# A fused attention, channel mixer and expert kernel: where gathers, output copies, transposes and index products stand in the order of work

## The chip, the cores and the metric

The kernel runs on one core of a Trainium2 chip. The metric is the device time of one execution in microseconds (us), from three runs of the same program. A profile of one further execution shows every instruction of the core's engines: PE (matrix products; PEld is its loading of the stationary operand), DVE, ACT and POOL (elementwise work), and the queues SP (plain transfers) and POOL (indirect transfers, those with a list of row numbers).

## The reference

Three stages follow one another on 4 batches of 576 tokens with 512 channels. The first is attention with 8 heads, in which scores further than `tau` below a row's maximum are dropped. The second adds a low-rank mix over tokens and a two-layer channel network:

```python
xt = x.transpose(0, 2, 1)
u = x + (xt @ U @ V).transpose(0, 2, 1)
x = u + np.maximum(u @ w_ch1, 0.0) @ w_ch2
```

The third sends each token to one of 8 experts (512 to 1024 to 512). A gate decides whether a token takes its own best expert or the expert of the token before it, so the choice runs along the tokens:

```python
fresh_e = int(np.argmax(logits[b, s]))
e = fresh_e if s == 0 or local_gate[b, s] < 0.5 else prev_e
out[b, s] = p[e] * (np.maximum(x[b, s] @ w1[e], 0.0) @ w2[e])
```

## The kernel before

**Stages.** Batch 0's attention runs alone. Then attention of batch b is interleaved with the channel network of batch b - 1 (`channel`, lines 633 to 642). At the end `channel(B - 1)`, the channel network of the last batch, runs interleaved with `early_slots` (line 886), which already plans two expert units from the first three batches' tokens. Then come the last batch's logits, the store of its rows to the DRAM buffer `ydram` (`store_rows`), its routing (`route`), the plan of the remaining units (`late_slots`) and the experts (`experts`, line 1127).

**Precision.** Every float32 product is made of three products of split operands: a high part, made by ACT (`h` in the names), and a remainder, made by DVE or POOL (`l`). So each weight chunk of 128x512 needs one ACT copy and one subtraction. For the channel weights (`load_w`, line 583) POOL makes all remainders: `w0l` and `w1l`, for the 16 slices f of the hidden layer. High and remainder parts of the first layer have two rooms (`W0`), those of the second five (`W1`). For the expert weights (`Chunks.split_to`, line 993) POOL makes one chunk's remainder in four (`k % 4 == 1`, line 1002), DVE the others. An expert unit has 16 chunks. Two of them share a raw buffer, which the SP queue refills for the next unit once both are split.

**Units and slots.** A slot is a list of up to 128 tokens of one expert, and a unit is one expert with one to three slots: unit 0 has 3, unit 1 has 2, the units after them 3, 3, 2, 2, 2, 2, 1, 1. `slot_rows` (line 817) makes the lists: for two groups of tokens at a time DVE builds a one-hot row matrix `r1` (96 tokens x 128 rows, line 858) and a narrow matrix `rh` with two columns for each slot (lines 861 to 867: the token number and the gate's probability). PE multiplies them into one PSUM bank, `pi` (line 869), over 18 token groups for units 0 and 1 (names ending in a) and 24 for the rest (ending in b). The narrow matrix is the stationary operand, so the result has a list in each row. It is copied (line 872), transposed by PE (line 874), copied again (line 878) and turned into integers (`idx`).

**A unit's way.** `gather` (line 1019) fetches a slot's rows from `ydram` by an indirect transfer on POOL's queue, into one of the six `wr` buffers, which the channel weights use too. `columns` (line 1037) transposes them on PE (`split_t`, line 1028): four transposes into one PSUM bank, then an ACT copy for the high part and a DVE subtraction for the remainder. Units 0 and 1 use the one bank `tp` of the pool `px`; later units use the two `mm` banks. `layer1` and `layer2` follow. `layer1` writes its sums to two `l1` banks in turn, so its third group has to wait until DVE has made the remainder of the first (`h_0l`, line 1074). `layer2` keeps one `l2` bank for each slot; there are three. Then each slot is scaled by DVE into an output tile `o` of 512 columns (line 1123), which takes one of two `yr` buffers, and written to the output by an indirect transfer on POOL's queue (line 1124). The third slot's `o` needs the buffer of the first, so it waits until that transfer has landed.

**Order.** Each engine takes its instructions strictly in the order in which they were queued. A planner works that order out beforehand from its own estimates of time: it takes the earliest-traced instruction that its clock holds to be ready. In the experts only SP keeps the order of the program. An instruction given to `keep_in_program_order` is queued behind the instruction traced last before it on its engine; this is order in the queue alone, no wait for an end.

The lines that matter for tracing order: all channel weights are traced before `experts`. There `gather(0)` is first, then `columns(0)`, then `gather(1)`, then unit 0's layer 1, in which unit 0's chunks are split. Of a channel slice `w0l` is traced before `w1l`, so the last POOL instruction traced before the gathers is `w1l` of slice 15.

Of the kernel before, what the change touches and what calls it, by code (L numbers as in the profile page):

```python
# [83 lines left out]
def attention_channel_moe(ctx, tc, qk, vv, tau, umat, vrep, wch, wgl, wexp, consts, out):  # L84
# [732 lines left out]
    def slot_rows(nm, nt, s0, s1):  # L817
# [29 lines left out]
            dve.tensor_reduce(out=slot, in_=sb, axis=AX.X, op=ALU.add)  # L847
        dve.tensor_tensor(out=slot, in0=slot, in1=q, op=ALU.add)
        bk = mm_tile if s0 else lambda n: px_tile("l2", n)
        pi = bk(f"pi{nm}")[:2 * n, :128]  # L850
        G = 2
        for j in range(0, nt, G):
            c = slice(j, j + G)
            bc = lambda x: x.unsqueeze(2).to_broadcast([CH, G, n])
            rf = me.tile([CH, G * 2 * NSLOT], F32, tag="rh", name=f"rh{nm}_{j}", bufs=2)
            rh = rf[:, :G * 2 * n].rearrange("p (g t s) -> p g t s", g=G, t=2)
            r1 = me.tile([CH, G, 128], F32, tag="r1", name=f"r1{nm}_{j}", bufs=2)
            dve.tensor_tensor(out=r1, in0=row[:, c].unsqueeze(2).to_broadcast([CH, G, 128]),
                              in1=cst[:CH, C_I128:C_I128 + 128].unsqueeze(1).to_broadcast([CH, G, 128]),
                              op=ALU.is_equal)  # L860
            for a, z, code in ((0, n, s0),) if s0 else ((0, FIRST[0], CODES[0]), (FIRST[0], EARLY, CODES[1])):
                m = z - a
                dve.tensor_tensor(out=rh[:, :, 1, a:z], in0=slot[:, c].unsqueeze(2).to_broadcast([CH, G, m]),
                                  in1=cst[:CH, C_SLOT + code:C_SLOT + code + m].unsqueeze(1).to_broadcast([CH, G, m]),
                                  op=ALU.is_equal)
            dve.tensor_tensor(out=rh[:, :, 0], in0=rh[:, :, 1], in1=bc(cst[:CH, C_TOK + j:C_TOK + j + G]), op=ALU.mult)
            dve.tensor_tensor(out=rh[:, :, 1], in0=rh[:, :, 1], in1=bc(p_all[:, c]), op=ALU.mult)
            for i in range(G):
                pe.matmul(pi, lhsT=rf[:, i * 2 * n:i * 2 * n + 2 * n], rhs=r1[:, i],
                          start=(j + i == 0), stop=(j + i == nt - 1))  # L870
        tr = me.tile([2 * NSLOT, 128], F32, tag="tr", name=f"tr{nm}")[:2 * n]
        dve.tensor_copy(tr, pi)
        pt = bk(f"pt{nm}")[:, :2 * n]
        pe.transpose(pt, tr, ident[:2 * n, :2 * n])
        ti = me.tile([128, 2, NSLOT], F32, tag="ti", name=f"ti{nm}", bufs=2)[:, :, :n]
        ii = me.tile([128, 2, NSLOT], F32, tag="ii", name=f"ii{nm}")[:, :, :n]
        idx = me.tile([128, 2, NSLOT], I32, tag="idx", name=f"idx{nm}", bufs=2)[:, :, :n]
        dve.tensor_copy(ti, pt.rearrange("p (a s) -> p a s", a=2))
        dve.tensor_scalar(out=ii[:, 0], in0=ti[:, 0], scalar1=-1.0, scalar2=0.0, op0=ALU.add, op1=ALU.max)
        dve.tensor_scalar(out=ii[:, 1], in0=ti[:, 0], scalar1=0.0, scalar2=OOB, op0=ALU.is_equal, op1=ALU.mult)  # L880
        dve.tensor_tensor(out=ii[:, 1], in0=ii[:, 0], in1=ii[:, 1], op=ALU.add)
# [87 lines left out]
    class Chunks:  # L969
# [23 lines left out]
        def split_to(self, n):  # L993
            while self.done < min(n, len(self.order)):
                s, k = self.order[self.done]
                hi, lo = self.room(f"{s}_{k}")
                self.done += 1
                i = k // 2
                x = raws[i][:, k % 2 * 512:k % 2 * 512 + 512]
                act.activation(hi, x, AF.Copy)  # L1000
                eng = pool if k % 4 == 1 else dve
                eng.tensor_tensor(out=lo, in0=x, in1=hi.bitcast(F32), op=ALU.subtract)  # L1002
                self.parts[s, k] = (hi, lo)
                if k % 2 and s + 1 < self.u1:
                    load_expert(s + 1, i)
# [13 lines left out]
    def gather(u):  # L1019
        for s in UNITS[u]:  # L1020
            yg = mlp.tile([128, DM], F32, tag="wr", name=f"yg{s}", bufs=WR)
            n = (B - 1) * S if s < EARLY else NTOK
            pool.indirect_dma_start(out=yg, out_offset=None, in_=ydram[:n, :],
                                    in_offset=bass.IndirectOffsetOnAxis(ap=ixs[s][0], axis=0),
                                    bounds_check=n - 1, oob_is_err=False)
            rows[s] = yg

    def split_t(name, src, hi, lo, late):

        tp = mm_tile(f"{name}p") if late else px.tile([128, 512], F32, tag="tp", name=f"{name}p")  # L1030
        for d in range(4):
            pe.transpose(tp[:, d * 128:d * 128 + 128], src[:, d * 128:d * 128 + 128], ident)
        t3 = tp.rearrange("p (a b) -> p a b", a=4)
        act.activation(hi, t3, AF.Copy)
        dve.tensor_tensor(out=lo, in0=t3, in1=hi.bitcast(F32), op=ALU.subtract)

    def columns(u):
# [6 lines left out]
        hi, lo = yts[u]  # L1044
        for i, s in enumerate(UNITS[u]):
            c = slice(i * 128, i * 128 + 128)
            split_t(f"y{s}", rows[s], hi[:, :, c], lo[:, :, c], u >= U0)
            yield

    def hidden(u, f):  # L1050
# [53 lines left out]
    def layer2(W, u, hs, nxt):  # L1104
# [14 lines left out]
        for _ in nxt:  # L1119
            pass  # L1120
        for i, s in enumerate(slots):
            o = mlp.tile([128, S], F32, tag="yr", name=f"o{s}", bufs=2)[:, :DM]
            dve.tensor_scalar(out=o, in0=po[i], scalar1=ixs[s][2], scalar2=None, op0=ALU.mult)  # L1123
            pool.indirect_dma_start(out=out, out_offset=bass.IndirectOffsetOnAxis(ap=ixs[s][1], axis=0),  # L1124
                                    in_=o, in_offset=None, bounds_check=NTOK - 1, oob_is_err=False)
# [119 lines left out]
```

## Time and profile before

| | |
|---|---|
| median of 3 runs | 1111.4 us (1111.2 to 1113.02) |
| the profiled execution | 1110.32 us |
| its span, first to last instruction | 1108.5 us |
| mean granted TensorE clock | 0.986 |
| busy share of the span | PE 94%, DVE 62%, ACT 52%, POOL 28% |

The profiled execution is 1.1 us below the median of the runs; 1.8 us of it lie outside the span. [...]

### The profile page before, as it was taken

What the parts mean: (1) busy time and instruction counts of PE and PEld (TensorE: products, weight loads), DVE (VectorE), ACT (ScalarE), POOL (GpSimd) and SP (SyncE); (2) the same over time, 40 slices, a digit from 0 to 9 for tenths busy, and PEclk for the clock granted to TensorE, in tenths of its full rate; (3) what the DMA queues carried; (4) which work ended last, traced back from release to release, by engine and by line L of the source; (5) the groups of instructions that cost most, each with busy time, mean ns of one, the idle gap of its engine ahead of it and who ended that gap; (6) DMA issues with size and microseconds to landing.
All of it is one profiled execution on the core that took longest, in us unless ns stands there. A gap on an engine that the chain in (4) does not pass through costs nothing. (4 is left out here: it accounts for less than half of the span.)

```text
span 1108.5 us, 19450 instructions
## 1 busy us (share of the span) xinstructions
PE 1037.1 (94%) x7170; PEld 910.7 (82%) x7170; DVE 687.5 (62%) x1617; ACT 581.6 (52%) x1220; POOL 313.4 (28%) x246
## 2 busy tenths in 40 slices
PE   6788899999999999999999999999999999999995
PEld 4566788889888889988898998979878788889874
DVE  6898776776465666646656554552458664456573
ACT  5788676674554556546464554332333344445462
POOL 1221123142222314221241222234411433233231
PEclk9899999999999999999999999989999999999998
DMA  6544577762223124132321211352243465456550
GB/s 199 184 152 138 181 247 227 240 214 93 88 92 95 58 78 126 53 99 77 94 70 42 67 49 55 114 213 82 77 138 133 129 222 162 153 175 200 186 170 15
DMA packets 57992, 143.83 MB, mean 130 GB/s; under 512 B 7133, under 2 KB 7901, under 8 KB 57888
## 3 DMA queue, kind: packets, MB, share of 16 engines
q1 hardware_dynamic: 54528, 132.27, 37.4%
q0 software_dynamic: 3360, 10.23, 2.8%
q8 instruction: 58, 0.95, 0.4%
q14 instruction: 46, 0.38, 0.1%
HBM read 124.65 MB, written 18.61 MB: 129 GB/s over the span
## 5 line engine op out<-in xcount | busy, mean ns | idle before, releaser
L610 PE MATMUL l<-uh,w0h 128*128 128x256 f32 (+1 forms) x512 | 157.9, 308 | 4.5 <-DVE hl L614 2.1
L596 POOL TENSOR_TENSOR w1l<-wr,w1h 128x512 fp32r<-128x512 f32 x64 | 81.7, 1299 | 269.7 <-ACT w1h L595 246.2
L627 PE MATMUL l<-hh,w1h 128*128 128x256 f32 (+1 forms) x512 | 157.4, 307 | 0.2 <-DVE yT L630 0.2
L612 PE MATMUL l<-uh,w0l 128*128 128x256 f32 (+1 forms) x512 | 153.7, 300 | 2.8 <-POOL w0l L596 2.8
L596 POOL TENSOR_TENSOR w0l<-wr,w0h 128x512 fp32r<-128x512 f32 x64 | 85.0, 1327 | 243.4 <-ACT w0h L595 233.8
L611 PE MATMUL l<-ul,w0h 128*128 128x256 f32 (+1 forms) x512 | 153.3, 299 | 0.0
L628 PE MATMUL l<-hl,w1h 128*128 128x256 f32 (+1 forms) x512 | 152.8, 298 | 0.0
L629 PE MATMUL l<-hh,w1l 128*128 128x256 f32 (+1 forms) x512 | 152.2, 297 | 0.0
L1000 ACT ACTIVATE eh<-ew 128x512 fp32r<-128x512 f32 x160 | 94.4, 627 | 88.6 <-PE el L1116 46.4
L335 ACT ACTIVATE p<-s,st 128x576 f32<-128x576 f32 x144 | 104.5, 741 | 61.3 <-DVE st L324 61.1
L1002 DVE TENSOR_TENSOR el<-ew,eh 128x512 fp32r<-128x512 f32 x120 | 98.4, 840 | 41.9 <-ACT eh L1000 40.6
L339 DVE SCALAR_TENSOR_TENSOR p<-s,st,p 128x576 f32<-128x576 f32 x144 | 114.6, 815 | 15.2 <-ACT p L335 10.0
L324 DVE TENSOR_REDUCE st<-s 128x1 f32<-128x576 f32 x144 | 105.6, 751 | 28.4 <-PE s L291 26.4
L289 PE MATMUL s<-kh,qs 128*128 128x288 f32 x320 | 99.7, 330 | 17.8 <-DVE p L339 8.4
L388 ACT ACTIVATE ptt<-tp 128x512 f32<-128x512 f32 (+1 forms) x192 | 90.3, 494 | 41.5 <-PE tp L387 41.1
L614 DVE SCALAR_TENSOR_TENSOR hl<-l,hh 128x256 fp32r<-128x256 f32 (+1 forms) x128 | 58.1, 454 | 81.3 <-ACT hh L613 80.6
L630 DVE TENSOR_TENSOR yT<-l,yT 128x256 f32<-128x256 f32 (+1 forms) x128 | 58.2, 455 | 77.9 <-PE l L629 77.4
L610 PEld LDWEIGHTS l<-uh,w0h 128*128 128x128 f32 x512 | 97.4, 190 | 8.3 <-DVE hl L614 3.4
L612 PEld LDWEIGHTS l<-uh,w0l 128*128 128x128 f32 x512 | 97.4, 190 | 4.1 <-POOL w0l L596 3.0
L627 PEld LDWEIGHTS l<-hh,w1h 128*128 128x128 f32 x512 | 97.0, 190 | 3.9 <-issue 2.6
L387 PE MATMUL tp<-cst,p 128*128 128x128 f32 x576 | 94.5, 280 | 5.0 <-ACT ptt L388 4.8
L1002 POOL TENSOR_TENSOR el<-ew,eh 128x512 fp32r<-128x512 f32 x40 | 55.3, 1383 | 153.0 <-ACT eh L1000 133.2
(467 smaller groups left out, 2526.7 us busy)
## 6 DMA issues: line engine op xcount, KB each, us to landing
ew<-in_wexp_dram SPq DMA_DIRECT2D x80, 512.0 KB, 4.3
wr<-wdram SPq DMA_DIRECT2D x128, 256.0 KB, 2.9
cr<-in_wch_dram SPq DMA_DIRECT2D x32, 512.0 KB, 5.0
raw<-in_qk_dram SPq DMA_DIRECT2D x30, 304.0 KB, 3.1
wdram<-w SPq DMA_DIRECT2D x32, 256.0 KB, 2.7
v<-in_vv_dram SPq DMA_DIRECT2D x16, 352.0 KB, 3.1
raw<-in_qk_dram SPq DMA_DIRECT2D x16, 320.0 KB, 3.6
raw<-in_qk_dram SPq DMA_DIRECT2D x17, 288.0 KB, 3.0
```

Source lines behind the costliest of these rows:

```text
L289: pe.matmul(s["t"][:, h, :288], lhsT=qs[:, qc:qc + 128], rhs=kh[:, k0:k0 + 288], start=(j == 0), stop=False)
L324: dve.tensor_reduce(out=self.st[:, 0, h:h + 1], in_=self.t[h], axis=AX.XY, op=ALU.max, negate=True)
L335: act.activation(self.halves(h), self.t[h], AF.Exp, bias=self.st[:, 0, h:h + 1])
L339: dve.scalar_tensor_tensor(out=p, in0=self.t[h], scalar=self.st[:, 1, h:h + 1], in1=p, op0=ALU.is_ge, op1=ALU.mult, accum_out=self.rvs[:, ...
L596: pool.tensor_tensor(out=lo, in0=x, in1=hi.bitcast(F32), op=ALU.subtract)
L610: pe.matmul(pm, lhsT=w1h[:, wk], rhs=uh[:, k, o:o + n], start=(k == 0), stop=False)
L611: pe.matmul(pm, lhsT=w1h[:, wk], rhs=ul[:, k, o:o + n], start=False, stop=False)
L612: pe.matmul(pm, lhsT=w1l[:, wk], rhs=uh[:, k, o:o + n], start=False, stop=(k == 3))
L627: pe.matmul(pm, lhsT=w2h[:, wd], rhs=hh[:, o:o + n], start=(f == f0), stop=False)
L628: pe.matmul(pm, lhsT=w2h[:, wd], rhs=hl[:, o:o + n], start=False, stop=False)
L629: pe.matmul(pm, lhsT=w2l[:, wd], rhs=hh[:, o:o + n], start=False, stop=(f == f0 + 3))
L1002: eng.tensor_tensor(out=lo, in0=x, in1=hi.bitcast(F32), op=ALU.subtract)
```

## The change

It has four parts.

1. In `gather`, unit 0's three gathers are kept in program order on POOL, and so are unit 0's four POOL remainders in `split_to`. The first gather is thereby queued behind `w1l` of slice 15, the first remainder behind the last gather of unit 1, and each of the others behind the one before it.
2. The third slot's output tile gets a buffer of its own in the pool `ma`.
3. The transposes of unit 0 go to the three `l2` banks; unit 1 keeps the bank `tp`, later units the `mm` banks.
4. In `slot_rows` the one-hot rows become the stationary operand and the narrow matrix the moving one. The result has the lists in columns, so the copy of line 872 and the transpose of line 874 with its bank are gone.

```diff
-        pi = bk(f"pi{nm}")[:2 * n, :128]
+        pi = bk(f"pi{nm}")[:, :2 * n]
...
-                pe.matmul(pi, lhsT=rf[:, i * 2 * n:i * 2 * n + 2 * n], rhs=r1[:, i],
+                pe.matmul(pi, lhsT=r1[:, i], rhs=rf[:, i * 2 * n:i * 2 * n + 2 * n],
                           start=(j + i == 0), stop=(j + i == nt - 1))
-        tr = me.tile([2 * NSLOT, 128], F32, tag="tr", name=f"tr{nm}")[:2 * n]
-        dve.tensor_copy(tr, pi)
-        pt = bk(f"pt{nm}")[:, :2 * n]
-        pe.transpose(pt, tr, ident[:2 * n, :2 * n])
...
-        dve.tensor_copy(ti, pt.rearrange("p (a s) -> p a s", a=2))
+        dve.tensor_copy(ti, pi.rearrange("p (a s) -> p a s", a=2))
...
-                eng.tensor_tensor(out=lo, in0=x, in1=hi.bitcast(F32), op=ALU.subtract)
+                x = eng.tensor_tensor(out=lo, in0=x, in1=hi.bitcast(F32), op=ALU.subtract)
+                if s == 0 and eng is pool:
+                    tc.keep_in_program_order(x)
...
-            pool.indirect_dma_start(out=yg, out_offset=None, in_=ydram[:n, :],
+            x = pool.indirect_dma_start(out=yg, out_offset=None, in_=ydram[:n, :],
...
+            if u == 0:
+                tc.keep_in_program_order(x)
...
-        tp = mm_tile(f"{name}p") if late else px.tile([128, 512], F32, tag="tp", name=f"{name}p")
+        tp = {0: lambda n: px_tile("l2", n), 1: lambda n: px.tile([128, 512], F32, tag="tp", name=n)}.get(
+            u, mm_tile)(f"{name}p")
...
-            o = mlp.tile([128, S], F32, tag="yr", name=f"o{s}", bufs=2)[:, :DM]
+            if i < 2:
+                o = mlp.tile([128, S], F32, tag="yr", name=f"o{s}", bufs=2)[:, :DM]
+            else:
+                o = ma.tile([128, DM], F32, tag="o", name=f"o{s}")
```

## Rows read from the trace of the kernel before

**Rows 1.** The page, part 1: busy us, share of the span, instructions.

```profile
PE 1037.1 (94%) x7170; PEld 910.7 (82%) x7170; DVE 687.5 (62%) x1617; ACT 581.6 (52%) x1220; POOL 313.4 (28%) x246
```

**Rows 2.** Timeline, PE, 870 to 980: start, us, engine, instruction [idle before <- releaser].

```profile
877.17 0.38 PE L1069 MATMUL el<-y1h,eh 128*128 128x256 f32 x1 [2.10 <-DVE h_0l L1074]
...
941.86 0.44 PE L1069 MATMUL el<-y3h,eh 128*128 128x384 f32 x1 [1.71 <-DVE h_0l L1074]
...
978.57 0.39 PE L1069 MATMUL el<-y4h,eh 128*128 128x256 f32 x1 [1.33 <-DVE h_1l L1074]
```

**Rows 3.** Timeline, the other engines, 868 to 877.

```profile
870.34 1.02 POOL L1124 DMA_INDIRECT out_dram<-o,idxa  x1 [0.16 <-DVE rhb L867]
...
873.69 0.39 ACT L1073 ACTIVATE h_0h<-el 128x256 fp32r<-128x256 f32 x1 [4.86 <-PE el L1071]
...
876.04 0.75 DVE L1123 TENSOR_SCALAR o<-el,tia 128x512 f32<-128x512 f32 x1 [2.88 <-DMA out_dram<-o,idxa]
...
876.70 0.41 DVE L1074 SCALAR_TENSOR_TENSOR h_0l<-el,h_0h 128x256 fp32r<-128x256 f32 x1
```

**Rows 4.** Timeline, all engines, 785 to 796.

```profile
788.14 1.02 POOL L1023 DMA_INDIRECT yg<-ydram,idxa  x1 [0.16 <-POOL w1l L596]
789.19 1.30 POOL L596 TENSOR_TENSOR w1l<-wr,w1h 128x512 fp32r<-128x512 f32 x1
789.28 0.63 ACT L595 ACTIVATE w0h<-wr 128x512 fp32r<-128x512 f32 x1 [1.28 <-PE l L611]
...
793.00 1.27 POOL L1002 TENSOR_TENSOR el<-ew,eh 128x512 fp32r<-128x512 f32 x1
...
793.16 2.88 DVE L1002 TENSOR_TENSOR el<-ew,eh 128x512 fp32r<-128x512 f32 x1 [1.50 <-ACT eh L1000]
794.22 1.26 POOL L596 TENSOR_TENSOR w0l<-wr,w0h 128x512 fp32r<-128x512 f32 x1
795.53 0.39 PE L612 MATMUL l<-uh,w0l 128*128 128x256 f32 x1 [2.75 <-POOL w0l L596]
```

**Rows 5.** Timeline, PE, 799 to 822: unit 0's transposes and first product.

```profile
800.03 0.49 PE L1032 MATMUL y0p<-cst,yg 128*128 128x128 f32 x3
...
819.86 0.66 PE L1032 MATMUL y2p<-cst,yg 128*128 128x128 f32 x4 [1.61 <-DVE y0l L1035]
...
821.20 1.01 PE L1069 MATMUL el<-y0h,eh 128*128 128x384 f32 x2 [0.69 <-ACT y0h L1034]
```

**Rows 6.** Windows: span, busy of PE PEld DVE ACT POOL, PEclk, DMA share, GB/s.

```profile
728.40:735.60 7.20, 7.14 (x30) 4.91 (x31) 4.69 (x17) 0.63 (x1) 2.73 (x2) 0.53 0.92 328
...
821.00:824.30 3.30, 3.10 (x12) 2.81 (x13) 0.69 (x1) 1.12 (x3) 0.00 (x0) 0.51 0.97 342
...
845.00:855.00 10.00, 9.39 (x43) 7.26 (x41) 9.97 (x34) 3.49 (x7) 2.46 (x2) 1.00 0.85 306
```

**Rows 7.** Timeline, PE, DVE and POOL, 719 to 730: the early index products.

```profile
722.42 1.28 POOL L1002 TENSOR_TENSOR el<-ew,eh 128x512 fp32r<-128x512 f32 x1 [11.94 <-ACT eh L1000]
...
722.47 1.25 DVE L866 TENSOR_TENSOR rha<-rha,cst 96x10 f32<-96x10 f32 x1
...
724.19 0.60 PE L869 MATMUL pia<-r1a,rha 96*10 96x128 f32 x4 [0.93 <-DVE rha L867]
...
725.88 3.98 POOL L596 TENSOR_TENSOR w1l<-wr,w1h 128x512 fp32r<-128x512 f32 x3 [2.19 <-ACT w1h L595]
...
728.45 0.64 PE L869 MATMUL pia<-r1a,rha 96*10 96x128 f32 x4 [1.56 <-DVE rha L867]
```

**Rows 8.** One line's instructions, L866: count, ns min/median/max, first and last start, form.

```profile
L866 DVE TENSOR_TENSOR rha<-rha,cst x9: 150/166/1282, 719.4 to 732.6; 96x10 f32<-96x10 f32 x9
```

**Rows 9.** Timeline, PE: 128 columns moving, then 9 columns moving.

```profile
719.85 1.04 PE L869 MATMUL pia<-r1a,rha 96*10 96x128 f32 x8
...
815.05 0.80 PE L662 MATMUL lg<-cst,lt 128*96 128x9 f32 x8
```

**Rows 10.** SP's timeline at 744: unit 1's first weights.

```profile
744.49 0.35 SPq L959 DMA_DIRECT2D ew<-in_wexp_dram  x1
```

**Rows 11.** Tile yg, 760 to 830: us from issue to landing.

```profile
DMA to landing us min/median/max: 3.3/3.4/3.5
```

More of the change, by code (lines that the diff above doesn't have):

```diff
@@ L1022, in gather, with split_t @@
             n = (B - 1) * S if s < EARLY else NTOK
-            pool.indirect_dma_start(out=yg, out_offset=None, in_=ydram[:n, :],
-                                    in_offset=bass.IndirectOffsetOnAxis(ap=ixs[s][0], axis=0),
-                                    bounds_check=n - 1, oob_is_err=False)
+            x = pool.indirect_dma_start(out=yg, out_offset=None, in_=ydram[:n, :],
+                                        in_offset=bass.IndirectOffsetOnAxis(ap=ixs[s][0], axis=0),
+                                        bounds_check=n - 1, oob_is_err=False)
+            if u == 0:
+                tc.keep_in_program_order(x)
             rows[s] = yg
-    def split_t(name, src, hi, lo, late):
-        tp = mm_tile(f"{name}p") if late else px.tile([128, 512], F32, tag="tp", name=f"{name}p")
+    def split_t(name, src, hi, lo, u):
+        tp = {0: lambda n: px_tile("l2", n), 1: lambda n: px.tile([128, 512], F32, tag="tp", name=n)}.get(
+            u, mm_tile)(f"{name}p")
         for d in range(4):
@@ L1046, in columns @@
             c = slice(i * 128, i * 128 + 128)
-            split_t(f"y{s}", rows[s], hi[:, :, c], lo[:, :, c], u >= U0)
+            split_t(f"y{s}", rows[s], hi[:, :, c], lo[:, :, c], u)
             yield
```

## The prediction

> **What bounds the kernel now.** I read the page's busy shares first: PE is busy for 94% of the span [rows 1], so time is lost only where PE stands still or runs at the lower clock. The windows by stage showed where that is from 715 us on, the part that the change touches. Then PE's timeline gave each stall with what ended it, and the timelines of the releasers why they were late. [...]
>
> In the experts PE stands still three times for a hidden remainder that DVE had not yet made: 2.10, 1.71 and 1.33 us [rows 2]. These are the first groups after a unit of three slots. The cause is one instruction ahead of it on DVE [rows 3]: the third output copy waits 2.88 us for the first slot's transfer, issued at 870.34, and the remainder `h_0l`, whose high part was begun at 873.69, stands behind it until 876.70. At 795.53 PE has waited 2.75 us for `w0l` of the last slice, whose high part ACT began at 789.28 but whose remainder POOL began only at 794.22 [rows 4]: gathers and an expert chunk stood ahead in POOL's queue. [...] Around 725 PE waits 0.93 and 1.56 us for the narrow matrices [rows 7], and then has 7.2 us at 0.53 [rows 6].
>
> **Third output room.** It takes away the wait of three copies, in units 0, 2 and 3. The copy itself (0.75 us) moves ahead of the hidden remainder. What is late next is that remainder's own chain: the high part ends at 873.69 + 0.39 = 874.08, the remainder at about 874.08 + 0.41 = 874.5 [rows 3]. PE came to its wait at 877.17 - 2.10 = 875.07 [rows 2], so the stall goes whole, with 0.6 us to spare. The output transfers remain in POOL's queue and still land one after another; POOL's remainders may wait there, but no PE stall of these rows is released by one. Gain 2.10 + 1.71 + 1.33 = 5.1 us; between 3.5 (each spare used up and half a microsecond more) and 5.1.
>
> **Pinned gathers and chunks.** The gathers move behind `w1l` of slice 15, but nothing puts them behind `w0l` of slice 15, which is traced before `w1l` and becomes ready after it. The planner let three entries pass between those two, the last of them the chunk at 793.00 [rows 4]; I expect three gathers there now. Then `w0l` comes earlier only by the gather that stood before `w1l`, 789.19 - 788.14 = 1.05 us [rows 4]. I take 1.1. Upper bound: `w0l` directly behind `w1l`, ready before PE asks, 2.75. Lower bound: `w1l` ends at 788.14 + 1.30 = 789.4, five gathers at 1.05 and the first pinned chunk at 1.27 go ahead, and `w0l` ends at 789.4 + 5.25 + 1.27 + 1.26 = 797.2 against 795.5, a loss of 1.7.
>
> The pins also move the first chunk's remainder from 722.42 to about 798. There it had blocked DVE: the product of line 866 beside it took 1.25 us [rows 7] against a median of 0.166 [rows 8], and PE's first wait of 0.93 us came 1.7 us later. I take 0.9 for it. The second wait stands beside three channel remainders that nobody moves, so I leave it, and the slow clock after it too. Bounds: if PE no longer falls to the lower clock, 0.93 + 1.56 + 7.2 x 0.47 = 5.9 us; if the slow stretch doubles, a loss of 3.4.
>
> [...]
>
> On SP's queue the refill of the first raw buffer, issued at 744.49 before [rows 10], now follows the moved chunk, at about 798. Unit 1's layer 1 is under way at 877 [rows 2], so it has over 70 us, and every channel load that the pins wait for stands ahead of it. Cost nothing; without that cover it would be the few microseconds of one landing.
>
> **Three banks for unit 0.** The third transpose no longer waits for the first bank's reader, so 1.61 + 0.69 = 2.3 us go if the planner brings all twelve transposes forward. The slow clock behind them cost 3.3 x 0.49 = 1.6; I take half, 0.8, since PE's work there stays thin (logits, row transposes). Against that, 845 to 855 has DVE at 9.97 of 10 us [rows 6]: routing and slot lists, which an earlier unit 0 does not shorten; I take 1.0 off. Gain 2.1; bounds 0 and 3.9.
>
> **Index products turned.** Each of the 18 + 24 products is two instructions. Eight with 128 moving columns take 1.04 us, eight with 9 moving and 96 stationary columns 0.80 [rows 9]: a gain of 0.03 each, 84 x 0.03 = 2.5 us at most. The new form loads 128 stationary columns; the nearest row with that many, the transposes, takes 0.66 for four [rows 5] against 0.60 for four index products [rows 7], a loss of 0.015 each, 1.3 us. [...] The dropped copy and transpose shorten the way to the row numbers, for which no PE wait stands in the rows; taken as 0 too.
>
> **The sum.** 5.1 + 1.1 + 0.9 + 2.1 + 0 = 9.2 us. Against the profiled execution's 1110.3 that is 1101.1; it lies 1.1 below the median, so the runs should give a median near 1102.0.
>
> **Rivals.** *The clock stays up as well.* The early wait goes whole, no stretch near 730 is slow, and the unit 0 stretch gains its bound: 1102.0 - (5.9 - 0.9) - (3.9 - 2.1) = 1095.2. For it: a POOL instruction that blocks DVE goes. Against it: the triple of `w1l` at 725.88 stays.
>
> *The pin misses its aim.* `w0l` falls behind all gathers and the chunk (2.8 worse than taken), and unit 0 gains nothing (2.1): about 1106.9. For it: no edge ties `w0l` to the gathers. Against it: the planner prefers earlier-traced work once ready.
>
> *Slower.* The planner queues unit 0's twelve transposes on PE, early since they now have banks, ahead of rows that have not landed. The gathers are later now: before, three transposes ran at 800.03 [rows 5], twelve microseconds after the gather at 788.14 [rows 4]; now I expect the third issue at about 793 to 795, and landing takes 3.4 us [rows 11]. If the transposes stand where PE is at 792.8, PE waits up to 5.6 us, and a slow stretch like that at 728 adds 3.4; the 2.1 of the three banks are not realised. That is 11.1 against the sum: 1113.1. It decides where transposes are queued ahead of about 798.
>
> [...]
>
> *No change.* DVE's full stage around 850 swallows what is won before it (1.1 + 0.9 + 2.1), and POOL's output transfers, now queued closer together, hold chunks so that some 4 of the 5.1 come back as other waits: about 1110.
>
> **Chances.** Forecast 0.52, clock up 0.15, pin misses 0.17, slower 0.09, no change 0.07. The range of 1095 to 1109.5 covers the first three and their bounds. A difference under 0.2% (2.2 us) is about what a measurement of this kernel can't tell from none. Faster 0.84, same 0.07, slower 0.09.
>
> **What would show it.** Output room: the third copy on DVE has no wait for a transfer, and PE no idle time before the third group of units 1, 3 and 4. Pins: on POOL the gathers stand behind the last `w1l`; the entries between it and the last `w0l` give the stall at that slice's products. Early products: the first long DVE product beside a POOL chunk is gone; PEclk from 728 to 736 tells which bound holds. Three banks: the last transpose has no idle before it, and PEclk near 822 is 1. The forecast is wrong if the three stalls return with another releaser, or if new idle time shows before transposes.

## The result and the profile after

| | us |
|---|---|
| before, median of the runs beside the changed kernel | 1112.21 |
| after, median (1101.44 to 1104.95) | 1101.99 |
| ratio after/before, 95% interval | 0.9897 [0.9874, 0.9921] |
| profiled execution after | 1102.38, span 1100.6, mean granted clock 0.983 |

By the medians the change is worth 10.2 us, by the ratio, which is not simply the quotient of the two medians (0.9908), 11.5; the two profiled executions lie 1110.32 - 1102.38 = 7.94 us apart, and so do their spans (7.9). The page's busy line of after, with the columns of [rows 1]: PE does the same work but for two instructions, yet it is busy 4.8 us less, although its mean granted clock fell from 0.986 to 0.983. So more than half of the 7.9 us is busy time and 3.1 us is idle time; where the busy time went shows in the second profiles further down.

```profile
PE 1032.3 (94%) x7168; PEld 915.2 (83%) x7168; DVE 685.7 (62%) x1615; ACT 580.9 (53%) x1220; POOL 313.9 (29%) x246
```

The waits of PE from 868 to 1000 us of after (who waited for whom: us in total, times, longest) are down to one; none of the three of [rows 2] is left.

```profile
PE y7p L1034 <- DVE y2l L1037: 1.2, 1, 1.2
```

The timeline of DVE and ACT of the same kernel shows why, beside [rows 3]: the third output copy waits for no transfer, and the hidden remainder follows its own high part.

```profile
869.69 0.74 DVE L1128 TENSOR_SCALAR o<-el,tia 128x512 f32<-128x512 f32 x1
870.58 0.39 ACT L1075 ACTIVATE h_0h<-el 128x256 fp32r<-128x256 f32 x1 [5.48 <-DVE rhb L866]
871.57 0.41 DVE L1076 SCALAR_TENSOR_TENSOR h_0l<-el,h_0h 128x256 fp32r<-128x256 f32 x1
```

PE's timeline of after from 794 to 870 (columns as in [rows 2]). The last transpose of unit 0 and the first expert product have no idle time before them, and the product starts 3.19 us earlier than in [rows 5]. But the wait for `w0l` has grown from 2.75 us [rows 4] to 3.97, and behind unit 0 the waits for DVE's routing (`rowb`, `rhb`) are longer: the one for `rowb` was 0.60 before, and those for `rhb` from 855 us on sum to 2.9 us where they were 1.3.

```profile
795.09 0.39 PE L612 MATMUL l<-uh,w0l 128*128 128x256 f32 x1 [3.97 <-POOL w0l L596]
...
815.78 0.63 PE L1034 MATMUL y2p<-cst,yg 128*128 128x128 f32 x4
...
818.01 0.60 PE L1071 MATMUL el<-y0h,eh 128*128 128x384 f32 x2
...
834.36 1.15 PE L722 MATMUL bk<-cst,rowb 1*96 1x1 f32 x12 [1.92 <-DVE rowb L717]
...
867.02 0.65 PE L869 MATMUL pib<-rhb,r1b 96*128 96x56 f32 x4 [0.98 <-DVE rhb L867]
```

POOL's timeline of after shows why the wait for `w0l` is longer, against [rows 4]: the gathers stand where they stood, one of them still ahead of the last `w1l`, and now two chunk remainders together, 2.49 us, stand ahead of `w0l`.

```profile
786.48 1.02 POOL L1021 DMA_INDIRECT yg<-ydram,idxa  x1 [0.15 <-POOL w1l L596]
787.52 1.30 POOL L596 TENSOR_TENSOR w1l<-wr,w1h 128x512 fp32r<-128x512 f32 x1
788.98 1.02 POOL L1021 DMA_INDIRECT yg<-ydram,idxa  x1 [0.16 <-POOL w1l L596]
790.30 1.00 POOL L1021 DMA_INDIRECT yg<-ydram,idxa  x1 [0.30 <-issue]
791.33 2.49 POOL L998 TENSOR_TENSOR el<-ew,eh 128x512 fp32r<-128x512 f32 x2
793.77 1.26 POOL L596 TENSOR_TENSOR w0l<-wr,w0h 128x512 fp32r<-128x512 f32 x1
```

A reason can be read from the instructions of the gather's line (count, ns min/median/max, first and last start): there are as many register moves on POOL's queue as transfers, 21, one ahead of each. Keeping an instruction in program order ties it to the one written before it on its engine, and for the gather that is then its own move. No run tests this reason by itself; that another kind of edge does move the gathers is shown further down.

```profile
L1021 POOLq MOVE  x21: 29/29/35, 769.1 to 986.2; - x21
```

At the early index products (POOL, DVE and PE of after, 721 to 728, beside [rows 7]) the chunk is gone from POOL, but a fourth `w1l` stands in its place. Beside each of the four, one operation of DVE that reads two tiles takes 0.92 to 1.26 us (the row of 1.33 holds two operations); in the kernel before there were five such, one beside each of the chunk and the four `w1l` there, of which [rows 7] shows the first. PE's two waits sum to 2.03 + 0.47 = 2.50 us where they were 0.93 + 1.56 = 2.49.

```profile
721.76 5.27 POOL L596 TENSOR_TENSOR w1l<-wr,w1h 128x512 fp32r<-128x512 f32 x4 [12.84 <-ACT w1h L595]
721.82 1.33 DVE L863 TENSOR_TENSOR rha<-ssta,cst 96x6 f32<-96x6 f32 x2
...
723.41 0.92 DVE L866 TENSOR_TENSOR rha<-rha,cst 96x10 f32<-96x10 f32 x1
...
724.59 1.22 DVE L867 TENSOR_TENSOR rha<-rha,p_all 96x10 f32<-96x10 f32 x1
...
725.87 0.61 PE L869 MATMUL pia<-rha,r1a 96*128 96x10 f32 x4 [2.03 <-DVE rha L867]
...
727.99 1.03 PE L869 MATMUL pia<-rha,r1a 96*128 96x10 f32 x4 [0.47 <-DVE rha L867]
```

The windows of after for three stretches (columns as in [rows 6]): the clock is at the lower level (0.50 from 731 to 734) for much of 730 to 743, and for a part of the time behind the longer wait for `w0l` (0.83; the window of the kernel before has 1.00 in this profile, but 0.84 in its second one, further down). At unit 0's transposes it now stays at 1.00, where the same window has 0.83 before.

```profile
730.00:743.00 13.00, 13.00 (x73) 13.00 (x72) 3.48 (x17) 2.98 (x7) 2.56 (x2) 0.68 0.39 139
790.00:800.00 10.00, 6.03 (x33) 5.82 (x33) 5.62 (x4) 2.19 (x5) 4.70 (x4) 0.83 0.53 157
815.00:825.00 10.00, 9.34 (x75) 8.12 (x68) 7.45 (x22) 7.08 (x16) 2.52 (x2) 1.00 0.77 238
```

PE's starts in the two profiles, before minus after, give the place of the gain: 1.6 us already near 703, where both kernels still run the same instructions on PE in the same order; -1.1 at unit 0's first transposes; +3.2 at unit 0's first product; +1.3 at unit 0's first product of layer 2 (844.44 and 843.13); +3.7 at the transposes of `y7p`; +6.4 at unit 4's first product, +7.9 at unit 5's, and no more from there.

### The profile page after: what moved, and what is told of

Same layout as the page of the kernel before. It is cut to its first block, busy times and chain, and to the rows that moved or that the text cites. A ratio compares the mean times of both kernels' runs of the same rounds, so it can differ in the third digit from the quotient of the medians.

```text
span 1100.6 us, 19448 instructions
## 1 busy us (share of the span) xinstructions
PE 1032.3 (94%) x7168; PEld 915.2 (83%) x7168; DVE 685.7 (62%) x1615; ACT 580.9 (53%) x1220; POOL 313.9 (29%) x246
## 4 chain that ended last, share of the span: by engine, by line
PE 69%; DVE 13%; ACT 7%; issue 5%; DMA 3%; POOL 1%; SPq 0%; POOLq 0%; ACTq 0%; DVEq 0%
PE l L627 5%; PE l L628 5%; PE l L629 5%; PE po L406 5%; PE l L610 5%; PE l L612 4%; PE l L611 4%; PE s L289 3%; PE tp L387 3%; PE el L1118 3%; PE el L1116 3%; PE el L1117 3%; PE el L1071 3%; PE el L1072 3%; PE el L1073 3%
## 5 line engine op out<-in xcount | busy, mean ns | idle before, releaser
L627 PEld LDWEIGHTS l<-hh,w1h 128*128 128x128 f32 x512 | 97.1, 190 | 3.6 <-issue 2.4
L611 PEld LDWEIGHTS l<-ul,w0h 128*128 128x128 f32 x512 | 99.2, 194 | 0.4
```

What stands on the lines that cost most here:

```text
L611: pe.matmul(pm, lhsT=w1h[:, wk], rhs=ul[:, k, o:o + n], start=False, stop=False)
L627: pe.matmul(pm, lhsT=w2h[:, wd], rhs=hh[:, o:o + n], start=(f == f0), stop=False)
```

## Experiments: each part alone

The theory from these rows is that the third room and the three banks carry the gain and that the pins and the turned products bring nothing. The rival is that the gain has another source, in a part that was priced at nothing. Each part alone tells them apart; the four ran on the same chip beside the kernel before, whose median there was 1114.61 us. A gain in us that stands behind a ratio is what the ratio lacks of 1, times that median.

**The third output room alone.**

```diff
-            o = mlp.tile([128, S], F32, tag="yr", name=f"o{s}", bufs=2)[:, :DM]
+            if i < 2:
+                o = mlp.tile([128, S], F32, tag="yr", name=f"o{s}", bufs=2)[:, :DM]
+            else:
+                o = ma.tile([128, DM], F32, tag="o", name=f"o{s}")
```

> The kernel before with the third output room alone. By the ledger of the two traces (three stalls of 2.10, 1.71 and 1.33 us before the third group of units 1, 3 and 4, and the order of work unchanged elsewhere) the time falls by 5 to 6.5 us and PE shows no idle time released by h_0l or h_1l in units 1, 3 and 4. Rival: the wait for the output transfers only changes its place, to POOL, whose late chunk remainders then stop PE; then the time falls by less than 2.5 us and PE shows new waits for POOL.

Measured: 1105.30 us, ratio 0.9917 [0.9899, 0.9935], so 9.2 us. The waits for `h_0l` and `h_1l` are gone in all three units. In unit 1 that brought little: from the first `pib` product to the transposes of `y7p` this profile takes 901.01 - 857.44 = 43.57 us and the one of before 899.41 - 855.66 = 43.75. The wait came back later in the same unit (PE's timeline):

```profile
886.27 0.38 PE L1069 MATMUL el<-y1h,eh 128*128 128x256 f32 x1 [1.91 <-issue]
```

The trace names no releaser; the row of DVE's remainder `h_5l` ends at 886.21, just before. In units 3 and 4 the gain is whole. A part of the 9.2 us can be clock: the six runs have a mean granted clock of 0.9845 and the kernel before 0.9827, and over the 55 runs of the kernel before that stand beside all these experiments a run with 0.001 less clock is 1.1 us longer, so an estimate from these runs is 2 us.

**The three banks alone.**

```diff
-        tp = mm_tile(f"{name}p") if late else px.tile([128, 512], F32, tag="tp", name=f"{name}p")
+        tp = {0: lambda n: px_tile("l2", n), 1: lambda n: px.tile([128, 512], F32, tag="tp", name=n)}.get(
+            u, mm_tile)(f"{name}p")
```

> The kernel before with unit 0's transposes in three banks alone. By the ledger (unit 0's first product 4.4 us earlier against the work around it, then 1.9 us given back at a wait for the routing row) the time falls by about 2.5 us. Rival: the whole 4.4 us stays, or DVE's full stage around 850 us eats all of it, so that the time falls by less than 1 us.

Measured: 1109.37 us, ratio 0.9964 [0.9945, 0.9983], so 4.0 us. As in the whole change, the last transpose (815.53) and the first product (817.76) have no wait before them; of the three waits of [rows 2] those in units 3 and 4 stand (1.9 and 1.6 us), and in unit 1 waits of 0.7 and 0.5 us at other places have taken the place of the 2.10.

**The turned index products alone.**

```diff
-                pe.matmul(pi, lhsT=rf[:, i * 2 * n:i * 2 * n + 2 * n], rhs=r1[:, i],
+                pe.matmul(pi, lhsT=r1[:, i], rhs=rf[:, i * 2 * n:i * 2 * n + 2 * n],
...
-        dve.tensor_copy(tr, pi)
...
-        pe.transpose(pt, tr, ident[:2 * n, :2 * n])
```

> The kernel before with the index products turned alone (one-hot rows stationary). As predicted: no change within 1.3 us either way, since the pace of the products stays at 0.11 us each. Rival: wider weight loads and narrower products lengthen the stretches at the lower clock at 730 and at 857 us, and the time rises by 1.5 to 3.5 us, with a granted clock under 1 in both.

Measured: 1105.67 us (1101.59 to 1111.06), ratio 0.9912 [0.9889, 0.9935], so 9.8 us. None of what was expected: the part that I had priced at nothing is worth as much as the third room. It is not a higher clock: over the runs of each the mean granted clock is 0.9825, and 0.9827 for the kernel before.

**The pins alone.**

```diff
+                if s == 0 and eng is pool:
+                    tc.keep_in_program_order(x)
...
+            if u == 0:
+                tc.keep_in_program_order(x)
```

> The kernel before with the pins alone. The prediction's theory: 2.0 us faster (1.1 at the last w0l, 0.9 in the early index products). Rival, from the trace after: the gathers keep their old places in POOL's queue, because each is pinned only behind its own register move, and the one thing that moves is the first chunk's remainder, into the place ahead of the last w0l; then PE's wait for w0l is about 4.0 us instead of 2.75, a stretch at the lower clock follows it, and the time rises by 1.2 to 3 us.

Measured: 1115.16 us, ratio 1.0005 [0.9988, 1.0022]: no gain, and of the rival's loss of 1.2 to 3 us only the lower end lies within the interval. POOL's order around the last `w0l` is that of the whole change, and so is the wait:

```profile
793.40 0.58 PE L612 MATMUL l<-uh,w0l 128*128 128x256 f32 x1 [3.97 <-POOL w0l L596]
```

Alone the parts sum to 9.2 + 4.0 + 9.8 - 0.6 = 22.4 us, twice what they bring together. So they share gains, and what a part is worth within the change needs the change without it.

## Experiments: the change without each part

Each is the whole change with one of the four diffs above taken back, as here the first; the kernel before ran beside them with a median of 1114.26 us. A part's worth is the ratio without it less 0.9897; with the intervals of both it is known to some 3 us, so the 3.0 of the three banks below is not clear of none.

```diff
-            if i < 2:
-                o = mlp.tile([128, S], F32, tag="yr", name=f"o{s}", bufs=2)[:, :DM]
-            else:
-                o = ma.tile([128, DM], F32, tag="o", name=f"o{s}")
+            o = mlp.tile([128, S], F32, tag="yr", name=f"o{s}", bufs=2)[:, :DM]
```

> The whole change without the third output room. Theory of the rows: the room is worth the stalls that it removes in units 1, 3 and 4, about 2.1 + 1.7 + 1.3 + 0.4 us, so this is 5 to 6 us slower than the whole change (about 1107.5 beside 1102, or 0.995 of the kernel before). Theory that the parts add up as they measured alone: 9.3 us slower than the whole change (about 0.999 of the kernel before). Its trace should show the waits for h_0l and h_1l of units 1, 3 and 4 again.

> The whole change without the three banks for unit 0's transposes. Theory of the rows: the banks win 4.4 us at unit 0's first product and give back 1.9 at the wait for rowb, so this is 2 to 3 us slower than the whole change. Theory of sums alone: 4.0 us slower. Rival: the early transposes only move the wait to DVE's later work, and this is within 1 us of the whole change. In the trace the wait for y0l before y2p (1.6 us) should be back and the wait for rowb should be 0.6 instead of 1.9.

> The whole change with the index products as they were (narrow matrix stationary, then a copy and a transpose). Alone the turned products were faster by about 9 us, where nothing had been expected. Theory that this is a gain of the turned form itself (no copy and no transpose between the last product and the indices): this is 4 to 9 us slower than the whole change. Theory that turning alone merely shifted the stretches in which the clock stands at half, by another order of the work around it: this is within 2 us of the whole change. In the trace the time from the first pib product to unit 1's first product should be about 16 us by the first theory and 13 by the second.

> The whole change without the pins. Theory of the rows: the pins left the gathers where they were and put one POOL remainder of unit 0's chunks ahead of the last w0l, so PE's wait for it was 3.97 us instead of 2.75 and the clock fell behind it; without them this is 1.2 to 3 us faster than the whole change (about 1099.5). By the prediction's own terms the pins were worth 2.0 us and this would be 2 us slower. Pins alone were within 0.5 us of the kernel before, so a difference under 1 us is the third possibility.

| without | median us | ratio to before | part worth, us | alone, us |
|---|---|---|---|---|
| third room | 1106.21 | 0.9940 [0.9921, 0.9959] | 4.8 | 9.2 |
| three banks | 1104.53 | 0.9924 [0.9903, 0.9944] | 3.0 | 4.0 |
| turned products | 1108.07 | 0.9946 [0.9926, 0.9965] | 5.5 | 9.8 |
| pins | 1102.88 | 0.9893 [0.9870, 0.9917] | -0.4 | -0.6 |

The theory that parts simply add falls, and so does the one that turning only shifted the slow stretches (5.5 us, where it allowed 2). Of the expected details, two missed: without the turned products unit 1's first product came 13.26 us after the first `pib` (875.98 - 862.72), where I had expected 16; and taking the pins away changed nothing, although the wait for `w0l` is 2.75 us again in that profile. In that execution the clock was lower around 735 (0.50 from 730 to 743, after 0.68); whether that is what takes the 1.2 us back in the other runs is not shown.

Without the third room PE's timeline has the waits of units 3 and 4 again, and none for `h_0l` in unit 1 (there a wait of 1.70 us stands later, as in the room alone):

```profile
937.26 0.44 PE L1071 MATMUL el<-y3h,eh 128*128 128x384 f32 x1 [1.68 <-DVE h_0l L1076]
944.24 0.44 PE L1071 MATMUL el<-y3h,eh 128*128 128x384 f32 x1 [0.44 <-DVE h_3l L1076]
973.95 0.39 PE L1071 MATMUL el<-y4h,eh 128*128 128x256 f32 x1 [1.31 <-DVE h_1l L1076]
```

From unit 3's first product to unit 5's this kernel takes 993.41 - 931.24 = 62.17 us and the whole change 990.10 - 932.16 = 57.94, so the room is worth 4.2 us there. Unit 1 is where the parts overlap: from the first `pib` product to `y7p` the stage takes 43.75 us before, 43.57 with the room alone, 40.45 with all but the turned products, 39.10 to 40.30 with the turned products alone, and 39.59 with everything (at a granted clock of 0.96 in the stage, the others at 1.00).

## Experiments: second profiles, and pins that hold

**The turned products alone, and the kernel before, a second time.** The edits are the one above, and none. Beside all kernels of this section the kernel before has a median of 1113.31 us.

> The turned index products alone, a second time, for a second profile: in the first the clock stood at half for 17 us around the early products, where the kernel before has 6.8, although the median was 9 us faster. If the gain is of the turned form, the median is again 7 to 10 us below the kernel before, and a profile near the median shows the early products without the long stretch at half clock, and unit 1's first product about 2.8 us closer to the first pib product. If it was chance, the median is within 3 us of the kernel before.

> The kernel before once more, for a second profile: its first profile, 1110.3 us, was among the fastest of its runs (median near 1114). If that profile was a lucky one in the stretch of the early index products, this one shows a longer stretch from the last row2b product to the first y0p transpose (95.4 us in the first) and more waits for rha or more time at half clock; the ratio is 1.000 within 0.2 per cent.

Measured: turned products 1106.71 us, ratio 0.9934 [0.9904, 0.9964], 7.3 us; the kernel before 1111.73, ratio 0.9991 [0.9972, 1.0011]. So a second set of runs shows the gain again. PE's timeline of the turned kernel shows that PE goes into unit 1's layer 1 while `pib` products are still to come, and the wait for `h_0l` of 2.10 us [rows 2] is gone.

```profile
869.46 0.28 PE L1065 MATMUL el<-y1h,eh 128*128 128x256 f32 x1
869.82 0.55 PE L869 MATMUL pib<-rhb,r1b 96*128 96x56 f32 x4
870.18 0.36 PE L1065 MATMUL el<-y1h,eh 128*128 128x256 f32 x1
```

DVE's timeline of the same kernel shows why: `h_0l` now stands ahead of the third output copy, which still waits for the first transfer; in [rows 3] it stands behind it. Which of the removed operations let the planner order it so is not shown.

```profile
871.94 0.42 DVE L1070 SCALAR_TENSOR_TENSOR h_0l<-el,h_0h 128x256 fp32r<-128x256 f32 x1 [0.92 <-ACT h_0h L1069]
...
873.29 0.75 DVE L1119 TENSOR_SCALAR o<-el,tia 128x512 f32<-128x512 f32 x1 [0.50 <-DMA out_dram<-o,idxa]
```

The stage from the first `pib` to `y7p` takes 43.75 us in the first profile of before, and 40.30 and 39.10 in the two of the turned form, all three at a granted clock of 1.00 (the second profile of before takes 45.41, at 0.96). Of these 3.5 and 4.6 us, idle time is only 0.9 and 1.6. The rest, 2.5 and 3.0 us, is time in which PE counts as busy, and most of it lies where PE changes between index products and others. PE and its weight loads in the kernel before, a group of four between expert products:

```profile
868.46 0.40 PE L1116 MATMUL el<-eh,h_7l 128*128 128x512 f32 x1
868.79 0.40 PEld L869 LDWEIGHTS pib<-r1b,rhb 96*56 96x56 f32 x4 [0.36 <-DVE rhb L866]
868.79 0.64 PE L869 MATMUL pib<-r1b,rhb 96*56 96x128 f32 x4
869.36 0.19 PEld L1114 LDWEIGHTS el<-eh,h_7h 128*128 128x128 f32 x1 [0.18 <-issue]
869.36 0.50 PE L1114 MATMUL el<-eh,h_7h 128*128 128x512 f32 x1
```

The same in the turned form, second profile:

```profile
862.08 0.39 PE L1112 MATMUL el<-eh,h_5l 128*128 128x512 f32 x1
862.09 0.64 PEld L869 LDWEIGHTS pib<-rhb,r1b 96*128 96x128 f32 x4
862.31 0.55 PE L869 MATMUL pib<-rhb,r1b 96*128 96x56 f32 x4
862.65 0.19 PEld L1110 LDWEIGHTS el<-eh,h_6h 128*128 128x128 f32 x1
862.68 0.48 PE L1110 MATMUL el<-eh,h_6h 128*128 128x512 f32 x1
```

From the expert product ahead of the group to the one behind it are 0.90 us before and 0.60 us turned. In the kernel before, the load of the group's first weights starts with the product itself (868.79 for both); in the turned form, where both kinds of product have 128 stationary columns, it starts 0.22 us ahead of the product (862.09 and 862.31). The data are not what the load waits for, though the row names an operation of DVE (it makes the next group's `rhb`): for the four groups at 862.23 to 866.65 in the kernel before, the last operation on their `rhb` had ended 0.7 us earlier.

The rest of the 7 to 10 us is not found in a profile. The profiles also compare unlike executions: those of the turned form had a granted clock of 0.977 and 0.981, below the 0.982 of its runs, and those of before 0.986 and 0.987, above the 0.983 of its runs. At the 1.1 us for 0.001 read above from the runs, that hides an estimated 8 us. One loss is visible in both profiles, where I had expected the second to be without it: a lower clock behind the early products. The window from 730 to 743 of the kernel before, second profile:

```profile
730.00:743.00 13.00, 11.46 (x73) 9.95 (x74) 5.75 (x23) 2.68 (x7) 3.59 (x3) 0.87 0.56 200
```

The same window of the turned form, second profile:

```profile
730.00:743.00 13.00, 13.00 (x66) 13.00 (x66) 4.01 (x20) 2.68 (x6) 1.85 (x2) 0.60 0.43 150
```

The first turned profile has 0.50 there. Over all profiles of these experiments, the eight with the turned form have 0.50 to 0.68 in this window; of the six without it, five have 0.78 to 0.87, and the change without the turned products has 0.61. So the lower clock goes with the turned form, but that form is not the only way to it. The second profile of before takes 801.72 - 704.66 = 97.1 us from the last `row2b` product to the first transpose, 1.7 more than the first; that is the direction expected, but less than half of the 4 us between the first profiled execution and the medians.

**Pins that hold.** The gathers of units 0 and 1 are queued behind the remainders `w1l` and `w0l` of slice 15 by an explicit edge; PE's order is that of the whole change.

```diff
+            LASTW[i:] = [y.ins]
...
+            with ExitStack() as pin:
+                if u < U0:
+                    for x in LASTW:
+                        pin.enter_context(tc.issue_after(x))
+                pool.indirect_dma_start(out=yg, out_offset=None, in_=ydram[:n, :],
```

> The whole change with the gathers of units 0 and 1 truly queued on POOL behind the remainders w1l and w0l of slice 15 (in the change as made they kept their old places ahead of them); TensorE's order is that of the whole change. What the prediction expected of the pins: w0l(15) comes at least one gather (1.05 us) earlier, here up to three, so PE's wait for it of 3.97 us falls to 1 us or less and the clock stays up behind it, and the time is 3 to 5 us below the whole change (ratio to the kernel before about 0.986). Rival: the gathers land later and PE waits for yg at the first transposes near 801 instead, by up to 2 us; then the gain is 1 to 2 us. Rival: nothing that is measurable, the wait for w0l is set by its load and not by POOL's queue.

Measured: 1104.19 us, ratio 0.9913 [0.9883, 0.9944]: no gain over the whole change (0.9897). The wait for `w0l` is gone, and one of 4.84 us stands in its place. POOL, SP, ACT, DVE and PE of this kernel, 791 to 808:

```profile
791.78 1.30 POOL L596 TENSOR_TENSOR w0l<-wr,w0h 128x512 fp32r<-128x512 f32 x1 [0.74 <-ACT w0h L595]
793.24 1.18 POOL L1026 DMA_INDIRECT yg<-ydram,idxa  x1 [0.17 <-issue]
...
800.14 2.56 POOL L999 TENSOR_TENSOR el<-ew,eh 128x512 fp32r<-128x512 f32 x2
...
801.48 1.57 SPq L956 DMA_DIRECT2D ew<-in_wexp_dram  x3
...
805.78 1.88 ACT L997 ACTIVATE eh<-ew 128x512 fp32r<-128x512 f32 x3 [6.82 <-DMA ew<-in_wexp_dram]
...
806.44 0.69 DVE L999 TENSOR_TENSOR el<-ew,eh 128x512 fp32r<-128x512 f32 x1 [3.19 <-ACT eh L997]
807.05 0.48 DVE L631 TENSOR_TENSOR yT<-l,yT 128x320 f32<-128x320 f32 x1
...
807.59 0.64 PE L628 MATMUL l<-hh,w1h 128*128 128x320 f32 x1 [4.84 <-DVE yT L631]
```

Read downwards: the pinned chunk remainder comes only after five gathers, at 800.14; it frees a raw buffer, so SP issues that buffer's refill at 801.48 (792.63 in the whole change); ACT waits for its landing; DVE has the next chunk's remainder in its queue ahead of `yT` of the last slice; PE waits for `yT`. Neither of my two rivals named this one.

**Pins that hold, and narrow matrices made with one tile read.** For the early products each operation with two tiles is split into two, one for each token chunk, that read one tile and a value per partition.

```diff
-            dve.tensor_tensor(out=rh[:, :, 1], in0=rh[:, :, 1], in1=bc(p_all[:, c]), op=ALU.mult)
+                for g in range(G):
+                    dve.tensor_scalar(out=rh[:, g, 1], in0=rh[:, g, 1], scalar1=p_all[:, j + g:j + g + 1],
+                                      scalar2=None, op0=ALU.mult)
```

> As the kernel with true pins, and the narrow one-hot matrices of the early index products are made with operations that read one tile and a value per partition, one for each token chunk, instead of operations that read two tiles. Theory that POOL's remainders (two tiles read) hold up just those of DVE's operations that read two tiles: each small operation stays at 0.1 to 0.2 us although POOL works beside it, the waits for rha of 2.03 and 0.47 us shrink to 0.5 or less, and the time is 1 to 4 us below true pins alone, more if the clock then stays up. Rival: every operation of DVE is held up while POOL works; then some of them take 0.9 to 1.3 us as before, the waits stay, and there are more operations to hold up, so the time is equal or up to 2 us worse.

Measured: 1107.02 us, ratio 0.9948 [0.9922, 0.9973], 2.8 us above true pins alone by the medians; the rival holds, at a little more than its price. The lines of this kernel that make the narrow matrices (ns, min/median/max):

```profile
L866 DVE TENSOR_SCALAR rha<-cst,ssta x36: 213/215/1339, 719.2 to 734.7; 96x3 f32<-96x3 f32 x18, 96x2 f32<-96x2 f32 x18
...
L874 DVE TENSOR_SCALAR rha<-rha,cst x18: 214/219/1323, 719.8 to 735.0; 96x5 f32<-96x5 f32 x18
L876 DVE TENSOR_SCALAR rha<-rha,p_all x18: 214/217/1303, 720.0 to 735.3; 96x5 f32<-96x5 f32 x18
```

At most they take 1.30 to 1.34 us, as long as the two-tile form (1.28 us in [rows 8]), by the median 0.22 us instead of 0.16 each, and there are twice as many: PE's longest wait for `rha` rose from 2.03 to 3.16 us. So the theory that an operation that reads one tile stays at 0.1 to 0.2 us beside POOL falls. No version of these beats the whole change beyond its interval; without the pins it is as fast and simpler.

## Why the prediction came out

The forecast of 1102.0 us and the measured 1101.99 agree, but so closely only by luck: the sum of 9.2 got there with one term that did not come and one that was missing (and 9.2 off the median of 1111.4 is 1102.2).

- **Third output room** (5.1): right, mechanism and size. It is worth 4.8 us within the change. The step that said that the stall of unit 1 goes whole, "with 0.6 us to spare", held for `h_0l`; but alone the room gained only 0.2 us of those 2.10, since a wait of 1.9 us came behind it in the same unit. Units 3 and 4 brought 4.2 where their rows promised 3.04. Of what else the room alone wins, 9.2 us by its runs, some 2 us can be their clock; the rest no profile shows.
- **Pins** (1.1 + 0.9): wrong. The step that failed is "The gathers move behind `w1l` of slice 15", and with it the sentence on the change that the first gather is queued there: the gathers stayed, most likely because each is tied to its own register move. What did move was a chunk remainder, into the place ahead of `w0l`, so the wait grew by 1.22 us, inside the lower bound given. The 0.9 at the early products failed too: a fourth `w1l` took the chunk's place on POOL. Both effects were in view: the first as the rival "the pin misses its aim" (its first half came: 1.2 us lost and 1.1 not won, 2.3 worse than taken where the rival had 2.8; unit 0 gained all the same), the second in [rows 7] and [rows 8], where an operation of DVE beside POOL's chunk took 1.25 us and its line's median is 0.166. In after, operations with a median of 0.153 to 0.159 us took 0.92 to 1.26 beside the four `w1l`. At the new place one remainder of DVE took 4.10 us (from 791.49; before, one took 2.88 [rows 4]), and no wait of PE came of it. "Cost nothing" for the refill of the raw buffer held for the change as made, where it goes out at 792.63, but was wrong for the pins as meant: with pins that hold it costs the 4.84 us above. I had looked for who needs the refilled chunk on PE and found 70 us of cover; the cover ended on DVE, whose queue has that chunk's remainder ahead of other work.
- **Three banks** (2.1): right in size. From the products `lt` (813.57 before, 814.74 after) to the first expert product the way is 1.17 + 3.19 = 4.4 us shorter. The two waits (1.61 and 0.69 us [rows 5]) are 2.30 of that; most of the rest is order, since eight row transposes (`py`, eight take 1.24 us) that stood ahead of this product now stand behind it. By layer 2, 1.9 us was lost again, with PE waiting for DVE (`rowb`, 1.92). That leaves 2.5, and by the runs it is 3.0, known to some 3 us, and 4.0 alone. Taking half for the slow clock (3.3 us at 0.51 [rows 6]) was my estimate and cautious; that PE's thin work there would keep the clock down is shown by no run: from 820 to 830 the granted clock is 1.00 in all seven profiles with the banks, and 0.83 in six of the seven without (1.00 in the second one of the kernel before). The loss that I put at 1.0 and between 845 and 855 came earlier and larger.
- **Turned products** (0, between -1.3 and +2.5): wrong, by 5.5 us within the change. The term was mis-sized in two steps. The first priced the products by their pace in a row of equal ones: "Eight with 128 moving columns take 1.04 us, eight with 9 moving and 96 stationary columns 0.80 [rows 9]". The 0 that the sum has for them, between the 2.5 and the -1.3, was my estimate, and no run shows it by itself: in a row of equal ones the pace held (eight early ones take 1.03 us after 1.04). But PE changes between groups of four and other products, and there the runs showed 0.60 us for a late group where it was 0.90: with the like beside it, 2.5 and 3.0 us in the stage of unit 1 of the two turned profiles. The second is "The dropped copy and transpose shorten the way to the row numbers, for which no PE wait stands in the rows; taken as 0 too". With them gone DVE makes `h_0l` ahead of the third output copy, which ends the wait that I had given to the third room. Within the change the room has ended that wait already, and the turned form shortens this stage by only 40.45 - 39.59 = 0.9 us, at the lower clock given above. So where most of the 5.5 comes from stays open.
- **Clock.** The sum left the slow stretch behind the early products as it was. From 730 to 743 the granted clock is 0.68 in after, and 0.78 and 0.87 in the two profiles of before, and the eight profiles with the turned form have 0.50 to 0.68; but the change without it has 0.61, and by the runs the turned form does not lower the mean clock (0.9825 and 0.9823, the kernel before beside these experiments 0.9827 to 0.9835).
- **The rivals.** The early waits and their slow stretch stayed, so the clock did not stay up; no transposes stood ahead of gathers that had not landed, so the slower case did not come. DVE took back 1.9 us of unit 0's gain and not all of it, and the waits of units 3 and 4 did not return under another name, so "No change" did not come either.

That the terms overlap (22.4 us alone, 10.2 to 11.5 together, 4.8 + 3.0 + 5.5 - 0.4 = 12.9 taken out one by one) was in no step. Part of the difference between the two profiles, 1.6 us near 703, is no effect of the change: two profiles of the turned kernel alone differ by 2.0 us there (704.78 and 702.74).

## What to carry to other kernels

A small product between large ones has to be priced with the changes on both sides of it, from the start of the large one ahead to the start of the large one behind, and not by its pace in a row of its own kind. An edit that removes dependent steps is worth what the scheduler does with the freed order, not only the price of the steps: when a stall stands near, ask whose place in the releasing engine's queue can change. When an instruction is pinned, read from the queue of the kernel as built whether it moved, and follow every buffer that it frees through the transfer to each engine whose queue holds the refilled data, not just to the engine that multiplies it. Two edits that cure the same stall are worth it once, so price sets of edits by stall and not by edit.

## What was not expected of the hardware

- Small operations of DVE that read one tile and a value per partition took 1.30 to 1.34 us at most beside POOL's remainders (a row of four in 4.96 us, 1.24 each), where their median is 0.215 to 0.219 us; this is the kernel with pins that hold and narrow matrices made with one tile read. In [rows 7] the operation that reads two tiles ends at 722.47 + 1.25 = 723.72, POOL's remainder beside it at 722.42 + 1.28 = 723.70.
- With 128 stationary columns instead of 10 the weight load of the early products takes 0.192 us in after instead of 0.092 before (medians), but eight products take 1.03 us after 1.04.
- Where PE goes from `pib` products to an expert product, the expert product starts 0.20 us after the last of them in the kernel before (56 stationary columns; eight times) and 0.09 us after it in the second profile of the turned form (128; ten times). No run changes the number of columns by itself.
